# A pad of NOPs on TensorE in three parts, and two weight loads behind a matmul: one change to a gated-linear-attention and feed-forward kernel

## The chip, the cores and the metric

The kernel runs on one core of a Trainium2 chip. The metric is the device time of one execution in microseconds (us), the median of several runs. A core has five engines that run their own instruction streams side by side: TensorE (PE; its weight loads are shown as PEld), VectorE (DVE), ScalarE (ACT), GpSimd (POOL) and SyncE (SP). Here SP asks for all the DMA transfers of data, in program order, on one queue.

## The reference

Two layers, one after the other. The first is a recurrent linear attention with a decay for every key channel; the second is a feed-forward layer with a squared ReLU.

```python
B, H, S, D = 4, 8, 768, 48
for t in range(S):
    state = alpha[:, :, t, :, None] * state + einsum('bhd,bhe->bhde', k[:, :, t], v[:, :, t])
    y[:, :, t] = einsum('bhd,bhde->bhe', q[:, :, t], state)
x = y.transpose(0, 2, 1, 3).reshape(B * S, H * D)      # 3072 x 384
h = maximum(x @ w_in, 0.0)                              # w_in 384 x 2048
out = (h * h) @ w_out                                   # w_out 2048 x 384
```

w_in and w_out come as 64-bit floats, q, k, v and alpha as 32-bit floats.

## The kernel before

**Blocks and groups.** The sequence is cut into chunks of 128 steps; a chunk of one batch element is a block n (24 blocks, n = 0 to 23). A block's attention is made of small products: `cs` (running sums of the logarithms of alpha), `turn` or `kT`/`qT` (transposes, tiles T, kT, qT), `scores` and `state_sums` (tile sckv), and `ga`/`gb` or `joined` (tile y). Four blocks make a group g of 512 rows of x (g = 0 to 5), and the feed-forward layer runs group by group: `ffn_in`, `half_in` or `layer_in` for h, and `layer_out` for the output.

**Products of two kinds.** In group 0, and in part of group 1, products are plain: one 32-bit product is two passes on TensorE. `out_plain` (line 832, products at L816, `o<-w_out,hid`) is such a stage, and in group 1 the first four of the eight pieces of w_out go through it. All other products of groups 1 to 5 use three parts of each factor: `in_x` (the parts a and l; L733, `h<-xa,wb` and `h<-xl,wl`), then `in_y` two steps later (the part d, `h<-xd,wd`). Between the two, ACT scales the sum: L748 or L750. The parts of the weights are made by ACT and DVE in group 1, stored in DRAM, and from then on they are streamed in by SP (L699, wl and wd) when a tile comes free.

**The order of work.** Nothing is scheduled at run time; the program is written out at build time. Up to the first whole products of group 0 a string (`AT['first']`) lists the steps, word by word: `fill1` is a product of zeros on TensorE (L395, tile zeros) whose result nobody reads, `weights3` asks for the next eighth of the weights (the number is not used: the pieces come in order), `load3v` asks for v of block 3, `first`, `middle` and `sga`/`sgb`/`sgc` are the steps in which DVE (L163, L167), ACT (L177, L180) and DVE (L187, L197, L206) turn a piece from 64-bit to 32-bit words. After that, `weave` runs through the list of products (units with a cost each) and puts the other steps (events with a due time) between them. A group's events are dated from `base[g]`, the sum of costs up to the group's start.

**The pad.** `align(place)` (line 1009) writes one instruction into TensorE's program that stands for as many NOPs as it takes until the next instruction is number `place` modulo 256. In the kernel before it is called from `attention`, 2.2 units ahead of the transposes of blocks 4, 14 and 16 (`AT['places']` and `AT['before']`). The three pads come to 59, 78 and 22 NOPs. The pad of 78 stands in group 2, between the sixth product of a step of `in_x` and the first product of the next `in_y`.

**The first SP transfers around the change** are, in order: a piece of w_in (the second), v_in of block 3, the third and the fourth piece of w_in, k_in, q_in and v_in of blocks 5, 4 and 4, and the fifth piece. `dep(later, earlier)` (line 489) makes one instruction wait for another on a semaphore.

Of the kernel before, what the change touches and what calls it, by code (L numbers as in the profile page):

```python
# [15 lines left out]


GB = 4
AT = {'v_by': (2.5, 3.5, 5.0), 'before': 2.2, 'places': ((4, 203), (14, 178), (16, 188)), 'evs': 0.65, 'lead': 4, 'post': 3, 'w_first': (45.25, 42.0, 55.95), 'wstep': 1.6, 'w_in_at': 2.5, 'w_in_by': 3.4, 'room1': 22, 'room': 25, 's0': 4, 'ahead': 6, 'late': 2, 'xs': 0.2, 'g0': ((1.5, 4, False, True, 28.25), (20.25, 6, True, True), (28.75, 8, True, False)), 'sc0': (2.35, 2.35, 2.35), 'g1': ((5.5, 8, False, 15.5), (15.5, 10, True), (34.5, 12, True)), 'g': ((1.7, 6, True), (15.5, 8, True)), 'g1x': 50.0, 'gx': 48.25, 'g0x': 55.25, 'k0': 2, 'h0': 16, 'k1': 4, 'h1': 3, 'h1by': 2, 'evs0': 0.3, 'tp': 'ADMD', 'tp1': 'ADAD', 'split': 8, 'o0': (44.75, 47.25), 'o1': (), 'o2': (21.75, 27.5, 31.75, 35.0, 41.25, 41.75), 'str1': 22.0, 'ga': 9.5, 'gb': 13.0, 'cv0': 1.5, 'first': 'ln0 warm0 cs0 load0v load2a ei0 load1v eb0 mk0 ln1 fill1 fill1 kT0 cs1 kc0 eb1 mq0 qT0 mq1 ei1 qc0 fill1 mk1 fill1 lt0 sc0 lt1 kT1 kv0 qT1 am0 ln2 weights2 us0 load2q kc1 qc1 cs2 sc1 fill1 am1 load2k ei2 load3a eb2 load4a fill1 kv1 st0 first0 us1 fill1 middle0 ln3 mq2 load3k ya0 qT2 yb0 mk2 fill1 qc2 kT2 cs3 kc2 load3q load2v weights5 sc2 eb3 load3v fill1 sga0 weights3 sgb0 fill1 ei3 ev0 mq3 mk3 am2 fill1 qT3 kT3 sgc0 first1 kc3 qc3 middle1 kv2 weights4 ha0 sc3 us2 kv3 sga1 ha1 am3 us3 sgb1 load4k ya2 load4q load4v first2 yb2 sgc1 middle2 weights6 lt3 ev2 lt2 st2 ha3 ha2 sgb2 sga2 hb1 sgc2 hb0 hb2 weights1 st1 hb3 st3 weights0'}


RUN = {0: 128, 32: 32, 64: 64, 96: 32}
# [3 lines left out]
def kernel(  # L26
# [12 lines left out]
    nc = tc.nc  # L39
# [41 lines left out]
    def two_k(name, dt=FP32, shape=(GB * C,)):  # L81
        return two_pool.tile([128, *shape], dt, tag="two", name=name)
# [12 lines left out]
    for x, n in (("q", 2), ("q", 3), ("k", 3)):  # L95
        t = lent[x, n] = two_k("qk_lent", shape=(H, 64))
# [29 lines left out]
    def load_weights(i):  # L126
        dt = moe_w_in.dtype
        shape = (KM, DF // NW) if i < NW else (NJ // NW, DM)
        if dt == FP32:
            raw = target(i)  # L130
        else:
            raw = raw_pool.tile([128, *shape], dt, tag="raw", name="raw")
        raws[i] = raw
        if i < NW:
            src = moe_w_in[:, i * DF // NW : (i + 1) * DF // NW]
            nc.sync.dma_start(out=raw, in_=src.rearrange("(k r) f -> r k f", r=128))
        else:
            i -= NW
            src = moe_w_out[i * DF // NW : (i + 1) * DF // NW, :]
            nc.sync.dma_start(out=raw, in_=src.rearrange("(j r) m -> r j m", r=128))  # L140


    half = {}
# [96 lines left out]
    last = consts.tile([128, 4, NP], FP32, name="last")  # L240
# [23 lines left out]
    def bank(n, name, shape=(NP, C)):  # L264

        return ps_att.tile([128, *shape], FP32, tag="att", name=name)
# [10 lines left out]

    SPLIT = AT["split"]

# [109 lines left out]
        (copied if n < GB else turned_copied)("k", n)  # L389


    def fill(k):
        ps = bank(0, "zeros", (2 * NP, 64))
        for _ in range(k):
            nc.tensor.matmul(  # L395
                out=ps[:, 0:NP, :], lhsT=s_t[3].rearrange("a p d -> a (p d)")[:, 0:128],
                rhs=s_t[3], start=True, stop=True,
            )
# [250 lines left out]
    here, todo, room = {}, [], [22]  # L649
# [28 lines left out]
    def diff_w(w, p):  # L678
# [97 lines left out]
    def splits_of_x(at, g):  # L776
        return [(at + i * AT["xs"], f, (g, i % KM)) for i, f in enumerate((split_x,) * KM + (diff_x,) * KM)]

    def layer_in(g):
        units = []  # L780
        for n in range(NJ + 2):
            if n < NJ:
                units.append((1.05, in_x, (n,)))
            if 0 <= n - 2 < NJ:
                units.append((0.53, in_y, (n - 2,)))
            if 0 <= n - AT["post"] < NJ:
                units.append((0, in_post, (n - AT["post"],)))
# [219 lines left out]
    places = dict(AT["places"])  # L1007
# [118 lines left out]
    for g in range(1, NG):  # L1126
        base.append(begin + sum(u[0] for u in units))
        at0 = base[g]
        units.append((0, begun, (g,)))
        units += layer_in(g) + layer_out(g)  # L1130
        units.append((0, ended, (g,)))
        if g + 1 < NG:
            for t, n0, after, *other in AT["g1"] if g == 1 else AT["g"]:
                n0 = n0 if g == 1 else n0 + GB * g
                other = [None if x is None else at0 + x for x in other]
                events += attention(at0 + t, n0, after, 1, True, *other)
            events += [(at0 + t, f, x) for t, f, x in splits_of_x(AT["g1x" if g == 1 else "gx"], g + 1)]
# [12 lines left out]

# [28 lines left out]
```

## Time and profile before

| | us |
|---|---|
| median of 3 runs | 522.24 (522.23 to 522.29) |
| the profiled execution | 521.93 |
| its span, from first to last instruction | 520.1 |
| TensorE busy in the span | 511.3 |
| DVE, ACT busy | 362.3, 315.6 |

TensorE's granted clock was 0.999 of full speed over the whole span. The profile is of one execution. A row of the timeline gives start, length, engine, line, operation, output and inputs, and in brackets how long the engine stood idle before it and which engine ended that idle time. "issue" means that the profile shows nothing that the engine waited for. PEldq is TensorE's sequencer. In group 0 to 5, L926 and L733 are the products into h, L816 those into the output.

### The profile page before, as it was taken

What the parts mean: (1) busy time and instruction counts of PE and PEld (TensorE: products, weight loads), DVE (VectorE), ACT (ScalarE), POOL (GpSimd) and SP (SyncE); (2) the same over time, 40 slices, a digit from 0 to 9 for tenths busy, and PEclk for the clock granted to TensorE, in tenths of its full rate; (3) what the DMA queues carried; (4) which work ended last, traced back from release to release, by engine and by line L of the source; (5) the groups of instructions that cost most, each with busy time, mean ns of one, the idle gap of its engine ahead of it and who ended that gap; (6) DMA issues with size and microseconds to landing.
All of it is one profiled execution on the core that took longest, in us unless ns stands there. A gap on an engine that the chain in (4) does not pass through costs nothing.

```text
span 520.1 us, 13202 instructions
## 1 busy us (share of the span) xinstructions
PE 511.3 (98%) x5350; PEld 421.9 (81%) x5350; DVE 362.3 (70%) x629; ACT 315.6 (61%) x664; POOL 5.3 (1%) x29
## 2 busy tenths in 40 slices
PE   8999999999999999989999999999999999999997
PEld 6775446668887669968899988899988899988997
DVE  3987979999879579757596466696465485363861
ACT  5678893687999566466953266962266863164620
POOL 4000000000000000000000000000000000000000
PEclk9999999999999999999999999999999999999999
DMA  9999686417888496998885796955683534798201
GB/s 185 214 269 253 180 209 180 67 61 231 242 229 199 121 279 162 309 306 227 183 238 163 245 268 185 227 174 163 214 273 123 182 123 153 252 355 294 70 0 62
DMA packets 139324, 102.36 MB, mean 197 GB/s; under 512 B 109808, under 2 KB 112896, under 8 KB 139264
## 3 DMA queue, kind: packets, MB, share of 16 engines
q1 hardware_dynamic: 139264, 101.52, 68.5%
q8 instruction: 43, 0.70, 0.5%
q14 instruction: 17, 0.14, 0.1%
HBM read 84.17 MB, written 17.33 MB: 195 GB/s over the span
## 4 chain that ended last, share of the span: by engine, by line
PE 92%; DVE 3%; ACT 2%; DMA 1%; issue 1%; SPq 0%; DVEq 0%; POOLq 0%
PE o L816 40%; PE h L733 31%; PE h L926 8%; PE y L409 4%; PE sckv L429 2%; PE T L586 2%; PE sckv L457 2%; DMA a_in<-in_alpha_dram 1%; ACT x L624 1%; PE cs L296 1%; PE cs L299 1%; PE cs L300 1%; DVE x L624 0%; DVE osb L656 0%; DVE xl L656 0%
## 5 line engine op out<-in xcount | busy, mean ns | idle before, releaser
L733 PE MATMUL h<-xa,wb 128*128 128x512 f32 x240 | 69.2, 396 | 0.0
L733 PE MATMUL h<-xd,wd 128*128 128x512 f32 x240 | 66.9, 394 | 1.8 <-ACT ha L706 1.7
L733 PE MATMUL h<-xl,wl 128*128 128x512 f32 x240 | 68.2, 392 | 0.0
L750 ACT ACTIVATE h<-h 128x512 f32<-128x512 f32 x40 | 23.3, 582 | 57.5 <-PE h L733 57.3
L656 DVE TENSOR_TENSOR hid<-h,hid 128x512 f32<-128x512 f32 x40 | 27.5, 688 | 42.7 <-PE h L733 39.9
L624 ACT COPY x<-y 32x256 f32<-32x256 f32 (+2 forms) x132 | 47.1, 364 | 15.2 <-PE y L409 13.0
L816 PE MATMUL o<-wb,ha 128*128 128x384 f32 x160 | 54.2, 339 | 0.0
L733 PEld LDWEIGHTS h<-xd,wd 128*128 128x128 f32 x240 | 44.4, 188 | 11.6 <-ACT ha L706 2.1
L816 PE MATMUL o<-wd,hd 128*128 128x384 f32 x304 | 53.7, 335 | 0.0
L816 PE MATMUL o<-wl,hl 128*128 128x384 f32 x160 | 53.6, 335 | 0.0
L816 PE MATMUL o<-w_out,hid 128*128 128x384 f32 x160 | 53.5, 490 | 0.0
L733 PEld LDWEIGHTS h<-xl,wl 128*128 128x128 f32 x240 | 44.9, 188 | 10.5 <-ACT wl L675 0.6
L816 PEld LDWEIGHTS o<-wd,hd 128*128 128x128 f32 x304 | 52.8, 188 | 0.0
L733 PEld LDWEIGHTS h<-xa,wb 128*128 128x128 f32 x240 | 44.3, 188 | 9.5 <-ACT xa L706 0.3
L816 PE MATMUL o<-wb,hx 128*128 128x384 f32 x144 | 48.8, 339 | 0.0
L816 PE MATMUL o<-wl,hx 128*128 128x384 f32 x144 | 48.2, 335 | 0.0
L816 PEld LDWEIGHTS o<-w_out,hid 128*128 128x128 f32 x160 | 30.0, 190 | 19.6
L926 PE MATMUL h<-x,w_in 128*128 128x512 f32 (+1 forms) x120 | 42.8, 510 | 0.2 <-DVE w_in L206 0.2
L706 ACT ACTIVATE ha<-hid 128x512 fp32r<-128x512 f32 x40 | 25.5, 636 | 23.8 <-DVE hx L656 13.1
L748 ACT ACTIVATE hid<-h 128x512 f32<-128x512 f32 x40 | 24.2, 606 | 25.2 <-PE h L733 25.1
L926 PEld LDWEIGHTS h<-x,w_in 128*128 128x128 f32 x120 | 22.5, 190 | 17.2 <-issue 14.2
L656 DVE TENSOR_TENSOR hl<-hid,ha 128x512 fp32r<-128x512 f32 x40 | 27.5, 686 | 11.2 <-ACT ha L706 11.2
(115 smaller groups left out, 883.7 us busy)
## 6 DMA issues: line engine op xcount, KB each, us to landing
wd<-do SPq DMA_DIRECT2D x36, 384.0 KB
wl<-lo SPq DMA_DIRECT2D x34, 384.0 KB
wl<-li SPq DMA_DIRECT2D x32, 384.0 KB
wd<-di SPq DMA_DIRECT2D x32, 384.0 KB
raw<-in_moe_w_in_dram SPq DMA_DIRECT2D x8, 768.0 KB
raw<-in_moe_w_out_dram SPq DMA_DIRECT2D x8, 768.0 KB
v_in<-in_v_dram SPq DMA_DIRECT2D x24, 192.0 KB
out_dram<-osb SPq DMA_DIRECT2D x24, 192.0 KB
```

Source lines behind the costliest of these rows:

```text
L409: ins = nc.tensor.matmul(out=ys[e][64 * half : 64 * half + D + G * e, m % 2, p // 2, t], lhsT=lhsT, rhs=rhs, start=(half, e) not in seen, ...
L429: nc.tensor.matmul(out=ps[e][HALF[h], 0, p, :], lhsT=ks[rows, p, HALF[h]], rhs=qs[rows, p, HALF[h]], start=True, stop=True, skip_group_che ...
L457: nc.tensor.matmul(out=ps[h][64 * e : 64 * (e + 1), 1, p, G:64], lhsT=tile_of("k", n)[HALF[h], 2 * p + e, :], rhs=tiles["v"][n % NV][HALF[ ...
L586: nc.tensor.transpose(out=ps[h][:, i, p, :], in_=rows[HALF[h], 128 * p : 128 * (p + 1)], identity=ident[HALF[h], HALF[h]],)
L624: copy(out=x[kk][to : to + m, t : t + 2], in_=blk[n]["y"][e][r : r + m, :, p // 2],)
L656: nc.vector.tensor_tensor(out=o, in0=x, in1=z, op=op)
L706: nc.scalar.activation(out=a, in_=x, func=AF.Copy, scale=NEAR)
L733: nc.tensor.matmul(out=acc["h", j], lhsT=here[w, "i", p][:, kk, jj * 128 : (jj + 1) * 128], rhs=x_parts[x][:, kk], start=start and kk == 0 ...
L748: nc.scalar.activation(out=hid[j], in_=x, func=AF.Copy, scale=E)
L750: nc.scalar.activation(out=x, in_=x, func=AF.Copy, scale=1.0 + E)
L816: nc.tensor.matmul(out=acc[t][:, 0:DM], lhsT=lhs[:, t * C : (t + 1) * C], rhs=rhs, start=start, stop=stop, skip_group_check=True,)
L926: nc.tensor.matmul(out=ps, lhsT=w[:, kk, c0 : c0 + 128], rhs=xT[g][kk][:, cols], start=(kk == 0), stop=(kk == KM - 1),)
```

## The change

It has two parts. In the first, `AT['places']` loses the entry for block 14, and a new tuple `pads` lists three calls of `align` as (group, time in the group, place): (1, 33.0, 218), (2, 0.5, 83) and (2, 5.5, 178). They are added to the events before `weave`. The last place, 178, is that of the old pad. In the second part, the word `weights3` leaves the list of first steps between `sga0` and `sgb0`, and a new word, `late0`, comes in behind `am2 fill1` and ahead of `qT3`. It asks for the same piece of w_in, the third, and makes that transfer wait for the last product of zeros written so far. For this, `load_weights` returns its DMA and `fill` keeps its last product. The order of the transfers on SP's queue stays the same.

```diff
-AT = {... 'places': ((4, 203), (14, 178), (16, 188)), ...
+AT = {... 'places': ((4, 203), (16, 188)), 'pads': ((1, 33.0, 218), (2, 0.5, 83), (2, 5.5, 178)), ...
-  'first': '... load3v fill1 sga0 weights3 sgb0 fill1 ei3 ev0 mq3 mk3 am2 fill1 qT3 kT3 ...'
+  'first': '... load3v fill1 sga0 sgb0 fill1 ei3 ev0 mq3 mk3 am2 fill1 late0 qT3 kT3 ...'
...
-            nc.sync.dma_start(out=raw, in_=src.rearrange("(k r) f -> r k f", r=128))
+            ins = nc.sync.dma_start(out=raw, in_=src.rearrange("(k r) f -> r k f", r=128))
...
+        return ins
...
+    zeros = {}
+
     def fill(k):
         ps = bank(0, "zeros", (2 * NP, 64))
         for _ in range(k):
-            nc.tensor.matmul(
+            zeros["last"] = nc.tensor.matmul(
...
+    steps["late"] = lambda _: dep(load_weights(to_load.pop(0)), zeros["last"])
...
+    events += [(base[g] + t, align, (place,)) for g, t, place in AT["pads"]]
     weave(units, sorted(events, key=lambda x: x[0]), begin)
```

More of the change, by code (lines that the diff above doesn't have):

```diff
@@ L18 @@
 GB = 4
-AT = {'v_by': (2.5, 3.5, 5.0), 'before': 2.2, 'places': ((4, 203), (14, 178), (16, 188)), 'evs': 0.65, 'lead': 4, 'post': 3, 'w_first': (45.25, 42.0, 55.95), 'wstep': 1.6, 'w_in_at': 2.5, 'w_in_by': 3.4, 'room1': 22, 'room': 25, 's0': 4, 'ahead': 6, 'late': 2, 'xs': 0.2, 'g0': ((1.5, 4, False, True, 28.25), (20.25, 6, True, True), (28.75, 8, True, False)), 'sc0': (2.35, 2.35, 2.35), 'g1': ((5.5, 8, False, 15.5), (15.5, 10, True), (34.5, 12, True)), 'g': ((1.7, 6, True), (15.5, 8, True)), 'g1x': 50.0, 'gx': 48.25, 'g0x': 55.25, 'k0': 2, 'h0': 16, 'k1': 4, 'h1': 3, 'h1by': 2, 'evs0': 0.3, 'tp': 'ADMD', 'tp1': 'ADAD', 'split': 8, 'o0': (44.75, 47.25), 'o1': (), 'o2': (21.75, 27.5, 31.75, 35.0, 41.25, 41.75), 'str1': 22.0, 'ga': 9.5, 'gb': 13.0, 'cv0': 1.5, 'first': 'ln0 warm0 cs0 load0v load2a ei0 load1v eb0 mk0 ln1 fill1 fill1 kT0 cs1 kc0 eb1 mq0 qT0 mq1 ei1 qc0 fill1 mk1 fill1 lt0 sc0 lt1 kT1 kv0 qT1 am0 ln2 weights2 us0 load2q kc1 qc1 cs2 sc1 fill1 am1 load2k ei2 load3a eb2 load4a fill1 kv1 st0 first0 us1 fill1 middle0 ln3 mq2 load3k ya0 qT2 yb0 mk2 fill1 qc2 kT2 cs3 kc2 load3q load2v weights5 sc2 eb3 load3v fill1 sga0 weights3 sgb0 fill1 ei3 ev0 mq3 mk3 am2 fill1 qT3 kT3 sgc0 first1 kc3 qc3 middle1 kv2 weights4 ha0 sc3 us2 kv3 sga1 ha1 am3 us3 sgb1 load4k ya2 load4q load4v first2 yb2 sgc1 middle2 weights6 lt3 ev2 lt2 st2 ha3 ha2 sgb2 sga2 hb1 sgc2 hb0 hb2 weights1 st1 hb3 st3 weights0'}
@@ new lines @@
+AT = {'v_by': (2.5, 3.5, 5.0), 'before': 2.2, 'places': ((4, 203), (16, 188)), 'pads': ((1, 33.0, 218), (2, 0.5, 83), (2, 5.5, 178)), 'evs': 0.65, 'lead': 4, 'post': 3, 'w_first': (45.25, 42.0, 55.95), 'wstep': 1.6, 'w_in_at': 2.5, 'w_in_by': 3.4, 'room1': 22, 'room': 25, 's0': 4, 'ahead': 6, 'late': 2, 'xs': 0.2, 'g0': ((1.5, 4, False, True, 28.25), (20.25, 6, True, True), (28.75, 8, True, False)), 'sc0': (2.35, 2.35, 2.35), 'g1': ((5.5, 8, False, 15.5), (15.5, 10, True), (34.5, 12, True)), 'g': ((1.7, 6, True), (15.5, 8, True)), 'g1x': 50.0, 'gx': 48.25, 'g0x': 55.25, 'k0': 2, 'h0': 16, 'k1': 4, 'h1': 3, 'h1by': 2, 'evs0': 0.3, 'tp': 'ADMD', 'tp1': 'ADAD', 'split': 8, 'o0': (44.75, 47.25), 'o1': (), 'o2': (21.75, 27.5, 31.75, 35.0, 41.25, 41.75), 'str1': 22.0, 'ga': 9.5, 'gb': 13.0, 'cv0': 1.5, 'first': 'ln0 warm0 cs0 load0v load2a ei0 load1v eb0 mk0 ln1 fill1 fill1 kT0 cs1 kc0 eb1 mq0 qT0 mq1 ei1 qc0 fill1 mk1 fill1 lt0 sc0 lt1 kT1 kv0 qT1 am0 ln2 weights2 us0 load2q kc1 qc1 cs2 sc1 fill1 am1 load2k ei2 load3a eb2 load4a fill1 kv1 st0 first0 us1 fill1 middle0 ln3 mq2 load3k ya0 qT2 yb0 mk2 fill1 qc2 kT2 cs3 kc2 load3q load2v weights5 sc2 eb3 load3v fill1 sga0 sgb0 fill1 ei3 ev0 mq3 mk3 am2 fill1 late0 qT3 kT3 sgc0 first1 kc3 qc3 middle1 kv2 weights4 ha0 sc3 us2 kv3 sga1 ha1 am3 us3 sgb1 load4k ya2 load4q load4v first2 yb2 sgc1 middle2 weights6 lt3 ev2 lt2 st2 ha3 ha2 sgb2 sga2 hb1 sgc2 hb0 hb2 weights1 st1 hb3 st3 weights0'}
@@ L139, in load_weights @@
             src = moe_w_out[i * DF // NW : (i + 1) * DF // NW, :]
-            nc.sync.dma_start(out=raw, in_=src.rearrange("(j r) m -> r j m", r=128))
+            ins = nc.sync.dma_start(out=raw, in_=src.rearrange("(j r) m -> r j m", r=128))
+        return ins
     half = {}
```

## The prediction

> **What bounds the kernel now.** I read the page first: which engine fills the span, and on which engine the chain that ended last runs.
>
> ```profile
> span 520.1 us, 13202 instructions
> PE 511.3 (98%) x5350; PEld 421.9 (81%) x5350; DVE 362.3 (70%) x629; ACT 315.6 (61%) x664; POOL 5.3 (1%) x29
> q8 instruction: 43, 0.70, 0.5%
> PE 92%; DVE 3%; ACT 2%; DMA 1%; issue 1%; SPq 0%; DVEq 0%; POOLq 0%
> ```
>
> TensorE is the bound: busy 511.3 of 520.1 us and 92% of the chain. The change removes no product, so all that it can win lies in the 8.8 us in which TensorE stands. The third line matters later: TensorE's program is fetched while it runs. 5350 products and 5350 weight loads, 159 NOPs and 136 waits that the program holds are 10,995 instructions, and 10,995 / 256 = 43, the number of packets on that queue (0.70 MB / 43 = 16 KB each). So one packet brings a block of 256 instructions, and a slot in the pad's code is a place in such a block.
>
> Next the waits of TensorE alone, longest first, and the chain in order of time (start, length, what).
>
> ```profile
> PE h L733 <- ACT ha L706: 1.7, 1, 1.7
> PE y L409 <- issue: 0.7, 1, 0.7
> ...
> 214.71 6.17 PE h L733 x27
> 296.08 6.17 PE h L733 x27
> 375.47 6.17 PE h L733 x27
> ```
>
> The two waits are the two places that the diff touches. The three chain rows are the starts of groups 2, 3 and 4. Group 2 lasts 296.08 - 214.71 = 81.37 us, group 3 lasts 79.39: the same work, 1.98 us apart.
>
> **Part 1: the pad.** First its NOPs (the rows of line 1011 in three stretches of time; count, then first and last start), then the timeline around the second pad, then busy time by stretch: the opening of groups 2, 3 and 4 up to the chain's T at 228.35, 307.76 and 387.15 (length, PE, PEld, DVE, ACT, POOL).
>
> ```profile
> L1011 PEldq NOP  x59: 13/13/13, 50.3 to 54.6; - x59
> L1011 PEldq NOP  x78: 13/13/13, 219.6 to 225.2; - x78
> L1011 PEldq NOP  x22: 13/13/13, 248.4 to 250.0; - x22
> ...
> 218.87 0.58 ACT L750 ACTIVATE h<-h 128x512 f32<-128x512 f32 x1 [0.76 <-PE h L733]
> 222.81 0.86 PE L733 MATMUL h<-xl,wl 128*128 128x512 f32 x3
> 225.35 0.94 PE L733 MATMUL h<-xd,wd 128*128 128x512 f32 x3 [1.68 <-ACT ha L706]
> ...
> 214.71:228.35 13.64, 11.96 (x54) 9.37 (x55) 7.42 (x15) 7.47 (x16) 0.00 (x0) 1.00 1.01 343
> 296.08:307.76 11.68, 11.68 (x54) 9.46 (x55) 6.82 (x15) 7.48 (x16) 0.00 (x0) 1.00 0.87 263
> 375.47:387.15 11.68, 11.68 (x55) 9.45 (x55) 6.82 (x15) 7.48 (x16) 0.00 (x0) 1.00 0.78 261
> ```
>
> A NOP costs the sequencer (225.2 - 219.6) / 77 = 0.073 us. The sequencer reaches the pad at 219.6 while TensorE still has products queued up to 222.81 + 0.86 = 223.67; so the queue covers about 223.7 - 219.6 = 4.1 us, and 78 NOPs last 5.7 us. The rest is the hole before 225.35. The profile names ACT's ha as releaser, because it ended just then (the pad's end is 225.2); but the product that comes next adds to the sum that ACT's L750 scaled at 218.87, 6.5 us earlier. I therefore put the hole down to the pad. The stretch rows price it without that argument: 13.64 - 11.68 = 1.96 us, and the two openings without a pad have TensorE busy in 11.68 of 11.68 us, with the same attention events and the same streamed weights. So what would be late next is known from group 3: nothing.
>
> Pieces of the new pad: the program holds 2805 TensorE instructions between the first pad (slot 203) and the new place at slot 218, then 863 to slot 83, then 69 to slot 178. 218 - 203 - 2805, 83 - 218 - 863 and 178 - 83 - 69 are each 26 modulo 256. So 78 = 26 + 26 + 26, each 26 x 0.073 = 1.9 us, and from slot 178 on every instruction stands where it stood. Whether 1.9 us is covered, piece by piece:
>
> ```profile
> 178.76 7.58 PE L816 MATMUL o<-w_out,hid 128*128 128x384 f32 x23
> 215.93 0.85 PE L733 MATMUL h<-xa,wb 128*128 128x512 f32 x3
> ```
>
> The first piece lies in the plain products, eight products (sixteen matmuls) ahead of cs at 185.9; one matmul there takes 7.58 / 23 = 0.33 us, so the same number of queued instructions covers more than behind 0.23 us products. It hides. The third is at the old place: 1.9 of 4.1 us. It hides. The second stands between the first and the second in_x, just ahead of the product at 215.93. There the sequencer has just passed the waits for the first loaded wl piece; if it was held there, the queue behind it is shorter than 4.1 us. From the 22 NOPs (1.6 us, 248.4 to 250.0) and the 59 NOPs (4.3 us) I take such lengths as hidden, and 0.6 us as what may show of the second piece. Term: -1.96 us, at worst -1.3.
>
> **Part 2: the order on the SP queue.** It keeps every transfer in its place; the third w_in piece now waits for the last of the zero products ahead of qT3, and behind it on that queue stand the fourth piece, then k_in, q_in and v_in of later blocks, and the fifth piece.
>
> ```profile
> 18.76 2.33 SPq L136 DMA_DIRECT2D raw<-in_moe_w_in_dram  x1
> 21.66 1.16 SPq L136 DMA_DIRECT2D raw<-in_moe_w_in_dram  x2
> 22.11 1.56 PE L395 MATMUL zeros<-s 128*128 128x256 f32 x6
> 29.41 0.33 PE L409 MATMUL y<-qs,us 48*48 48x64 f32 x7
> 29.84 0.55 DVE L163 TENSOR_SCALAR power<-raw 128x768 uint32<-128x768 uint32 x1
> 30.49 0.58 PE L409 MATMUL y<-qs,us 48*64 48x64 f32 x25 [0.75 <-issue]
> 30.49 0.44 PEld L409 LDWEIGHTS y<-qs,us 48*48 48x48 f32 x24 [0.88 <-issue]
> 32.42 2.65 DVE L624 COPY x<-y 32x256 f32<-32x256 f32 x6 [0.69 <-PE y L409]
> 32.86 0.32 ACT L357 COPY last<-lastT 48x4 f32<-48x4 f32 x2 [0.71 <-PE lastT L350]
> 33.10 3.07 PE L926 MATMUL h<-x,w_in 128*128 128x256 f32 x13
> ...
> 22.00:24.00 2.00, 2.00 (x24) 1.73 (x16) 1.96 (x6) 1.92 (x6) 0.00 (x0) 1.00 0.86 259
> 24.00:26.00 2.00, 1.78 (x40) 1.47 (x39) 1.91 (x5) 1.62 (x5) 0.00 (x0) 1.00 1.13 335
> 26.00:28.00 2.00, 2.00 (x70) 1.56 (x68) 1.57 (x3) 1.97 (x4) 0.00 (x0) 1.00 1.07 394
> ...
> q8 instruction: 1, 0.02, 34.0%
> q8 instruction: 1, 0.02, 92.8%
> ```
>
> The last two rows are the DMA queues of 27.8 to 28.0 and of 31.6 to 31.7 (share of 16 engines): a fetch that starts at about 27.9 and takes 0.34 x 16 x 0.2 = 1.09 us, and one at 31.6 of 0.928 x 16 x 0.1 = 1.48 us. Counted back from slot 203, the product at 30.49 is the first instruction of a block. So the 0.75 us "issue" is TensorE waiting for its program: the block was fetched at 27.9 to 29.0 and ran 1.5 us later. The block before it began among the six zeros matmuls, at 22.3 to 22.6, so its successor was due to be asked for then, and got its turn 5 us later. In between, the DMA engines were full (335 and 394 GB/s in the stretches from 24 and 26 on) with the second and the third w_in piece, asked for at 18.76 and 21.66. With the third asked for only after 22.11 + 1.56 = 23.67, 2.0 us later, the fetch stands ahead of it; it should then start at about 26 and be usable at 26 + 1.1 + 1.5 = 28.6, before 29.5. The hole goes: 0.75 us of TensorE idle, 0.88 us by the weight loads.
>
> How much of it stays won has two limits. TensorE's next users do not all follow: the x copies on DVE and the copy on ACT waited 0.69 and 0.71 us for TensorE, so they can come at most 0.7 us earlier. And the next block's fetch is itself just in time: 31.6 + 1.48 + up to 1.5 = 34.6 us, while its first instruction, 256 on, is the seventh of the h products, at 33.10 + 6.5 x 0.215 = 34.5 us. If TensorE arrives 0.9 us earlier and that fetch does not move, TensorE waits there again. It is asked for at the crossing, which moves from 30.49 to about 29.5, but into the tail of the delayed fourth piece. Between 0 and -0.9 us I take the middle, -0.45.
>
> The delay itself I cost at nothing. From 22.0 on the engines still have the second piece (0.79 MB) and a v load (0.20 MB): 0.52 MB go by 24.0, the rest at 335 GB/s by 25.4, so the queue hardly runs dry before the third piece, asked for at 23.7, arrives. It then lands near 26 + 0.79 / 0.38 = 28.1 us, and DVE reads it at 29.84. Without that cover DVE's conversions would be late and each us of it would cost up to one us at the next h products.
>
> [...]
>
> **Sum.** -1.96 - 0.45 = -2.4 us on the profiled execution, 521.93 to 519.5; it is 0.31 us below the median of the runs, so 522.24 becomes 519.8 us. Three runs lie within 0.06 us; a change under 0.2% (1.0 us) counts as none.
>
> **Rivals.**
> *The fetch stays late* (the next block takes the gain back, or the third piece was not what held it): only part 1 counts, 522.24 - 1.96 = 520.3. For it: the just-in-time fetch at 31.6. Against it: 5 us from crossing to fetch just while the w_in pieces fill the engines. Chance 0.25. [...]
> *The blocks' borders move into a bad place.* Between the first and the second piece all instructions stand 26 slots later, so four borders (in program order near 186, 198, 204.5 and 210.6 us) fall 26 instructions earlier in the work. One that is reached before its fetch, as at 30.49, costs 0.75 to 0.9 us: 520.7. Against it: each of these blocks lasts 6 us or more, because each holds long products. Chance 0.06.
> *The hole is ACT's,* as the profile's releaser has it: then parting the pad wins nothing there, and only part 2 counts, 522.24 - 0.45 = 521.8. Chance 0.03: groups 3 and 4 have the same ACT work (7.48 us in the stretch) and no hole. [...]
> *The NOPs are not covered* (slower): if the sequencer is held by a wait right ahead of each piece, the queue is empty and each shows its whole 1.9 us: 5.7 in place of 1.96, 522.24 + 3.7 = 526.0. It decides from two uncovered pieces on; one alone (1.9) leaves about today's time. For it: the second piece follows waits for loads. Against it: the first and the third stand in steady products. Chance 0.05 for slower, 0.03 for one piece.
>
> The forecast has the remaining 0.58. The range runs from 522.24 - 1.3 = 520.9, part 1 at its worst and nothing from part 2, to both holes in full, 522.24 - 1.98 - 0.9 = 519.4, widened by the 0.3 us between profile and median: 519.0 to 520.9, rounded down. Faster 0.89 (the forecast and the first two rivals), same 0.06 (ACT's hole, one piece uncovered), slower 0.05.
>
> **What would show it.** Right: line 1011 in three lots of 26 in group 1's plain products, at the opening of group 2 and at the old place, with TensorE's busy time equal to the stretch; group 2 as long as group 3; no "issue" row at y L409 and an instruction packet at about 26. Wrong: a PE wait at h L733 near 216 or 222, a new "issue" row at h L926 near 34, or a DVE L163 that waits for raw.

## The result, and the profile after

The changed kernel takes 521.03 us (median of 22 runs, 520.10 to 523.05); the kernel before, run beside it, 522.34 (521.88 to 524.17). The ratio is 0.9975, interval 0.9966 to 0.9984: 1.3 us faster, where 2.4 were forecast, and just outside the range of 519.0 to 520.9. In two later comparisons the ratio was 0.9973 (0.9959 to 0.9988) and 0.9972 (0.9961 to 0.9983). The profiled execution took 520.71 us, 1.22 less than that of before.

Line numbers of the changed kernel: L395, L409, L487, L586, L733, L816, L926 and L1011 became L398, L412, L490, L589, L736, L819, L929 and L1016. The page first (span, busy time, shares of the chain):

```profile
span 518.9 us, 13202 instructions
PE 512.0 (99%) x5350; PEld 422.0 (81%) x5350; DVE 362.1 (70%) x629; ACT 316.2 (61%) x664; POOL 5.3 (1%) x29
PE 93%; DVE 2%; ACT 2%; DMA 1%; SPq 0%; issue 0%; POOL 0%; DVEq 0%; POOLq 0%
```

TensorE is still the bound. The NOPs of the three pieces, each from a stretch of its own (count, first and last start):

```profile
L1016 PEldq NOP  x26: 13/13/13, 176.0 to 177.9; - x26
L1016 PEldq NOP  x26: 13/13/13, 213.5 to 215.3; - x26
L1016 PEldq NOP  x26: 13/13/13, 220.0 to 221.8; - x26
```

The starts of groups 2, 3 and 4 in the chain:

```profile
214.90 6.35 PE h L736 x27
294.88 6.17 PE h L736 x27
374.26 6.17 PE h L736 x27
```

Busy time by stretch for the openings of groups 2 and 3 (length, PE, PEld, DVE, ACT, POOL, clock, DMA share, GB/s):

```profile
214.90:226.76 11.86, 11.86 (x54) 9.37 (x55) 6.92 (x15) 7.49 (x16) 0.00 (x0) 1.00 0.98 341
294.88:306.56 11.68, 11.68 (x55) 9.44 (x55) 6.82 (x15) 7.47 (x16) 0.00 (x0) 1.00 0.89 265
```

The three pieces are where they were meant to be, and in this execution none shows: TensorE is busy in 11.86 of 11.86 us. The opening lost 13.64 - 11.86 = 1.78 us. But group 2 now starts at 214.90, 0.19 later than before, and from T to the end of the span there are 518.9 - 226.76 = 292.14 us, where there were 520.1 - 228.35 = 291.75: 0.39 longer. 1.78 - 0.19 - 0.39 = 1.20, the difference of the spans. Group 2 as a whole lasts 294.88 - 214.90 = 79.98 us and group 3 79.38, where the prediction had them equal. So one reading gives two losses, one ahead of group 2 and one behind its opening. Both have rows. The start, weight loads that TensorE waited for (start, length, in brackets the idle time):

```profile
29.44 0.69 PEld L412 LDWEIGHTS y<-qs,us 48*48 48x48 f32 x32 [0.33 <-issue]
34.65 1.91 PEld L929 LDWEIGHTS h<-x,w_in 128*128 128x128 f32 x9 [0.98 <-issue]
```

The hole at 30.49 is gone (the 0.33 at 29.44 was there before as well), and in its place stands one of 0.98 us at the h products, exactly one block of 256 instructions later. Behind the opening, in group 2's second stretch of attention:

```profile
239.25 0.36 DVE L490 TENSOR_TENSOR s<-s,last 128x192 f32<-128x192 f32 x1 [2.88 <-DMA last<-row]
239.53 0.68 DVE L768 SCALAR_TENSOR_TENSOR hid<-hid 128x512 f32<-128x512 f32 x1
240.13 0.68 DVE L659 TENSOR_TENSOR hid<-h,hid 128x512 f32<-128x512 f32 x1
```

And TensorE in the same timeline:

```profile
240.87 0.96 PE L736 MATMUL h<-xa,wb 128*128 128x512 f32 x3 [0.21 <-DVE hid L659]
```

VectorE waits 2.88 us for `last`, the decay row of block 14 or 15, which goes to DRAM and back; everything behind it on VectorE is late, and TensorE, which needs the buffer that L659 frees, loses 0.28 us there (0.42 from one product to the next, usually 0.14). In the kernel before, VectorE waited 1.68 us at the same place and TensorE nothing:

```profile
239.65 0.36 DVE L487 TENSOR_TENSOR s<-s,last 128x192 f32<-128x192 f32 x1 [1.68 <-DMA last<-row]
```

### The profile page after: what moved, and what is told of

Read it like the earlier page. It is cut to its first block, busy times and chain, and to the rows that moved or that the text cites. A ratio compares the mean times of both kernels' runs of the same rounds, so it can differ in the third digit from the quotient of the medians.

```text
span 518.9 us, 13202 instructions
## 1 busy us (share of the span) xinstructions
PE 512.0 (99%) x5350; PEld 422.0 (81%) x5350; DVE 362.1 (70%) x629; ACT 316.2 (61%) x664; POOL 5.3 (1%) x29
## 4 chain that ended last, share of the span: by engine, by line
PE 93%; DVE 2%; ACT 2%; DMA 1%; SPq 0%; issue 0%; POOL 0%; DVEq 0%; POOLq 0%
PE o L819 40%; PE h L736 31%; PE h L929 7%; PE y L412 4%; PE T L589 2%; PE sckv L432 2%; PE sckv L460 2%; DMA raw<-in_moe_w_in_dram 1%; ACT x L627 1%; PE cs L297 1%; PE warm L251 1%; PE cs L301 1%; PE cs L300 1%; SPq L119 0%; DVE osb L659 0%
## 5 line engine op out<-in xcount | busy, mean ns | idle before, releaser
L736 PE MATMUL h<-xa,wb 128*128 128x512 f32 x240 | 69.1, 396 | 0.2 <-DVE hid L659 0.2
L736 PE MATMUL h<-xl,wl 128*128 128x512 f32 x240 | 68.1, 392 | 0.0
L736 PE MATMUL h<-xd,wd 128*128 128x512 f32 x240 | 66.9, 394 | 0.1
L659 DVE TENSOR_TENSOR hid<-h,hid 128x512 f32<-128x512 f32 x40 | 27.5, 688 | 41.2 <-PE h L736 38.4
L819 PE MATMUL o<-wb,ha 128*128 128x384 f32 x160 | 54.2, 339 | 0.0
L819 PE MATMUL o<-wd,hd 128*128 128x384 f32 x304 | 53.7, 334 | 0.0
L819 PE MATMUL o<-w_out,hid 128*128 128x384 f32 x160 | 53.5, 490 | 0.0
L819 PE MATMUL o<-wl,hl 128*128 128x384 f32 x160 | 53.5, 334 | 0.0
L736 PEld LDWEIGHTS h<-xl,wl 128*128 128x128 f32 x240 | 44.9, 188 | 10.5 <-ACT wl L678 0.6
L819 PEld LDWEIGHTS o<-wd,hd 128*128 128x128 f32 x304 | 52.8, 188 | 0.0
L736 PEld LDWEIGHTS h<-xd,wd 128*128 128x128 f32 x240 | 44.4, 188 | 9.9 <-ACT hid L751 0.8
L736 PEld LDWEIGHTS h<-xa,wb 128*128 128x128 f32 x240 | 44.3, 188 | 9.8 <-ACT xa L709 0.3
L819 PE MATMUL o<-wb,hx 128*128 128x384 f32 x144 | 48.7, 338 | 0.0
L819 PE MATMUL o<-wl,hx 128*128 128x384 f32 x144 | 48.1, 334 | 0.0
L819 PEld LDWEIGHTS o<-w_out,hid 128*128 128x128 f32 x160 | 29.9, 190 | 19.7
L929 PE MATMUL h<-x,w_in 128*128 128x512 f32 (+1 forms) x120 | 42.9, 510 | 1.0 <-ACT x L627 0.8
L929 PEld LDWEIGHTS h<-x,w_in 128*128 128x128 f32 x120 | 22.5, 190 | 18.2 <-issue 15.9
L659 DVE TENSOR_TENSOR hl<-hid,ha 128x512 fp32r<-128x512 f32 x40 | 27.4, 686 | 10.9 <-ACT ha L709 10.8
```

The lines of the kernel that those rows point to most:

```text
L659: nc.vector.tensor_tensor(out=o, in0=x, in1=z, op=op)
L736: nc.tensor.matmul(out=acc["h", j], lhsT=here[w, "i", p][:, kk, jj * 128 : (jj + 1) * 128], rhs=x_parts[x][:, kk], start=start and kk == 0 ...
L819: nc.tensor.matmul(out=acc[t][:, 0:DM], lhsT=lhs[:, t * C : (t + 1) * C], rhs=rhs, start=start, stop=stop, skip_group_check=True,)
L929: nc.tensor.matmul(out=ps, lhsT=w[:, kk, c0 : c0 + 128], rhs=xT[g][kk][:, cols], start=(kk == 0), stop=(kk == KM - 1),)
```

## The experiments

Ratios are to runs of the kernel before beside them on the same chip; 0.001 is 0.52 us, and the brackets hold 95% intervals. Each kernel has one profiled execution. A border is the step in TensorE's program from one block of 256 instructions to the next (in the kernel before, 43 packets of 16,384 bytes brought 10,995 instructions, 255.7 each). "Border stalls" are the idle times of the weight loads put down to "issue" at the y products near 30 us and the h products near 34.5 or a little later (without the 0.33 that all kernels show).

**One part alone.** The two parts apart:

```diff
 pads alone:   'first': the word weights3 back at its old place, no late0
 delay alone:  'places': ((4, 203), (14, 178), (16, 188)), 'pads': ()
```

> The pad in three parts alone; the third w_in piece is asked for at its old place. Theory A (the pad's hole is gone in full; what was lost is at the start, where the next block's fetch takes the first hole's gain back): 522.3 - 1.9 = 520.4 us, runs as close together as those of before (0.4 us), the hole of 0.75 us at y L412 near 29.7 still there, and TensorE without a wait at h L736 near 223. Rival B (the pad's pieces or the borders that moved in group 1 cost something again): 521.2 us or more, with a wait on TensorE between 180 and 230 us or runs spread over 2 us.

> The late third piece alone; the pad of 78 NOPs is whole at its old place. Theory A: 522.3 us within 0.3 in the middle, but runs spread over 1.5 to 2 us, because the length of the new hole near 34 us hangs on when that block's fetch gets its turn; the hole at 223 is there with 1.7 us. Rival B: 521.5 us (0.75 us won at 29.7 and kept), runs close together.

Pads alone: 521.93 us, 0.9989 (0.9975 to 1.0002). Delay alone: 522.96 us, 0.9998 (0.9985 to 1.0011), border stalls 0 and 1.64. So the delay by itself shows no gain (its interval still holds the 0.45 us forecast), and the pads by themselves bring less than 1.96. The two gains together, 0.0011 and 0.0002, make half of the changed kernel's 0.0025 to 0.0028; the intervals are too wide to tell whether that is noise. Why the pads alone bring less, their profile shows. The NOPs of its middle piece:

```profile
L1016 PEldq NOP  x26: 13/13/13, 215.6 to 217.5; - x26
```

and TensorE around them:

```profile
214.84 0.86 PE L736 MATMUL h<-xa,wb 128*128 128x512 f32 x3
215.59 0.92 PE L736 MATMUL h<-xl,wl 128*128 128x512 f32 x3
217.59 0.94 PE L736 MATMUL h<-xa,wb 128*128 128x512 f32 x3 [1.08 <-issue]
```

Here the middle piece begins at 215.6, when TensorE is already in the products with the first streamed wl piece, and shows 1.08 us; in the profile above it began at 213.5 and showed nothing.

**The third piece, the fourth piece, and the loads behind them.** The fourth piece behind the first y product of block 2, too:

```diff
-  ... kv2 weights4 ha0 ... sgb1 load4k ya2 load4q load4v first2 ...
+  ... kv2 ha0 ... sgb1 ya2 behind2 load4k load4q load4v first2 ...
```

> The changed kernel, and the fourth w_in piece (and the k, q and v loads behind it) is asked for only behind the first y product of blocks 2 and 3, that is after the border at 29.5 us. Theory A: the fetch of the next block starts at about 30.3 in place of 31.9, the 0.74 us wait at h near 34 is gone, and the time falls to about 519.8 us with runs close together. Rival B, and a rival C by which a fetch takes its 1.5 us and more whatever stands beside it: the wait near 34 stays and the time is that of the changed kernel, 521.0 us. If the loads behind are then late, a wait for a_in near 45 us or for raw shows.

522.75 us, 0.9991 (0.9977 to 1.0006). The first fetch started at 28.12 (27.29 in the profile of the changed kernel) with a stall of 0.62, although the fourth piece no longer stood there. The second border stalled for 2.07 us, the longest stall of all these kernels. Two stretches of this kernel (the two last numbers are the DMA share and GB/s):

```profile
28.00:31.00 3.00, 2.51 (x66) 1.89 (x61) 2.64 (x6) 1.54 (x5) 0.00 (x0) 1.00 0.04 11
31.00:34.00 3.00, 2.87 (x110) 2.58 (x100) 2.50 (x6) 2.52 (x6) 0.00 (x0) 1.00 0.84 264
```

From 28 to 31 us the DMA engines were all but empty. The fourth piece was asked for at 30.07, k_in, q_in and v_in from 30.53 on; TensorE crossed the border at 30.55, and the fetch started at 34.22 only. By then the fourth piece had been moved (264 GB/s over the second stretch are its 0.79 MB, and it landed at 34.19 to 34.80; the trace has a record for each of the sixteen shares of a transfer), while the three loads landed at 35.28 to 38.37. So this fetch went behind the fourth piece, which had been asked for half a microsecond ahead of the border, and not behind the three loads.

Then the same three loads and the fifth piece, asked for only behind the third h tile:

```diff
-  ... sgb1 load4k ya2 load4q load4v first2 yb2 sgc1 middle2 weights6 lt3 ev2 lt2 st2 ha3 ha2 ...
+  ... sgb1 ya2 first2 yb2 sgc1 middle2 lt3 ev2 lt2 st2 ha3 held0 load4k load4q load4v ha2 ...
```

> The changed kernel, with k_in, q_in and v_in of blocks 5, 4 and 4 and the fifth piece of w_in asked for only when the last product of the third h tile has run (about 34.3 us; before, they were asked for from 24.7 us on). The third and fourth piece stay as they are. Theory A, the next block's fetch waits behind those small transfers: it starts near 29.8 to 30.5 us in place of 31.9, the stall at the h products near 33.5 (0.74 us) goes, and TensorE reaches 46 us some 0.5 to 0.7 us earlier; the time falls by as much, unless the fifth piece, then landing near 38 us, comes too late for VectorE. Theory B, the fetch is not held by transfers but asked for at about 31.8 us whatever is on the queues: it starts at 31.6 to 32.3 as in all runs so far, the stall stays at 0.7 us or more, and the time is the same or longer.

524.09 us, 1.0028 (1.0016 to 1.0041), and yet the second fetch came early, as theory A has it. The instruction packet in the DMA queues of 29.8 to 30.0 us:

```profile
q8 instruction: 1, 0.02, 33.9%
```

and the waits of 44 to 64 us (total, times, longest):

```profile
ACT a_in L275 <- DMA a_in<-in_alpha_dram: 5.0, 1, 5.0
PEld h L929 <- DVE w_in L207: 2.2, 1, 2.2
...
PE T L589 <- DVE q_in L316: 0.9, 1, 0.9
```

The second fetch started at 29.91 (31.86 in the changed kernel), both border stalls were 0, and cs came at 45.53 (46.27). What was moved then came too late itself: alpha's transfer, the fifth piece and q. Against two other kernels that crossed the first border without a stall, with the first fetch nearly as early (25.23 and 25.65, here 24.83) but the three loads asked for ahead of the border, the second fetch is 1.5 us earlier (31.45 and 31.44 there).

**The middle piece and the row transfers.** The changed kernel again, as a mark; the middle piece 24 instructions later; the row transfers on GpSimd's queue:

```diff
 middle later:     'pads': ((1, 33.0, 218), (2, 2.5, 107), (2, 5.5, 178))
 rows on GpSimd:   q = nc.gpsimd if n in (14, 15) else nc.sync      # in bl and br
                   q.dma_start(...)
```

> The changed kernel once more, as the mark for the other three runs. Its gain was about 1.3 us, not 2.4. If its spread comes from the second piece of the pad (shown in full when the first streamed wl piece lands late, hidden otherwise), the profiled execution shows either a hole of about 1.2 us at 216 us or none. In both cases: the start's two stalls at block borders together 0.8 to 0.9 us (y near 29.5 and h near 33.5), and about 0.3 to 0.5 us more than usual between sckv and h near 240.4. Time 521.0, 0.9975 of before.

> The changed kernel, with the middle piece of 26 NOPs one step of in_x later (behind the second one, not behind the first); the two other pieces and all other instructions as in the changed kernel. Theory, the middle piece is only partly covered because the sequencer has just been held by the wait for the first streamed wl piece: 24 instructions later it has its queue again, no hole near 216 in any execution, time 0.3 to 0.6 us below the changed kernel and a narrower spread. Rival, the middle piece is hidden as it stands and the gain is lost elsewhere: the same time as the changed kernel, 521.0, and the same spread.

> The changed kernel, with the four small transfers that bring the last decay row of blocks 14 and 15 to DRAM and back asked for by GpSimd's own queue, in place of SP's, which at that time stands behind a streamed wl piece. Theory, that round trip is what is late next when the pad's hole is gone: VectorE's wait for last<-row near 239 us (2.9 us in the changed kernel, 1.7 before) falls under 1 us, the 0.28 us that TensorE loses near 240.4 goes, time 0.3 us below the changed kernel. Rival, the small transfers are late because the DMA engines are full and not because of SP's queue: the wait stays between 2 and 3 us and the time as it is.

Again: 521.06 us, 0.9973. The same program, now with the hole: its middle piece, the product behind it, and the opening by stretch.

```profile
L1016 PEldq NOP  x26: 13/13/13, 215.3 to 217.3; - x26
```

```profile
217.33 0.94 PE L736 MATMUL h<-xa,wb 128*128 128x512 f32 x3 [0.88 <-PE h L736]
```

```profile
214.90:227.90 13.00, 12.12 (x55) 9.53 (x56) 7.11 (x15) 7.55 (x16) 0.00 (x0) 1.00 0.95 324
```

Middle piece later: 520.82 us, 0.9969 (0.9955 to 0.9983), no hole near 216, and nine of twelve runs within 520.5 to 521.1, where the mark spread from 520.0 to 523.4. The medians differ by 0.24 us in the expected direction, which the intervals do not tell apart. Rows on GpSimd: 520.95 us, 0.9973 (0.9959 to 0.9987). VectorE's wait for `last` is gone, and so is TensorE's loss (the lines of these kernels stand two further down):

```profile
236.26 0.36 DVE L492 TENSOR_TENSOR s<-s,last 128x192 f32<-128x192 f32 x1
```

```profile
240.44 0.97 PE L738 MATMUL h<-xa,wb 128*128 128x512 f32 x3
```

So that round trip was late because of SP's queue. TensorE's loss follows the length of the wait: at 1.68 us (the kernel before) and at 2.32 (the loads behind h, and the second mark further down) it lost nothing, at 2.9 to 3.1 (six profiles) it stood 0.21 to 0.45 us. By the times the repair shows nothing: 520.95 and the mark's 521.06 are one within the noise. Its profiled execution was the shortest of all, 520.51 us. The same edit in the kernel before:

> The kernel before, with nothing changed but the row transfers of blocks 14 and 15 on GpSimd's queue. Theory, this wait costs TensorE nothing as long as the pad's hole stands ahead of it: VectorE's wait for last<-row (1.7 us) goes and the time stays within 0.2 us of before. Rival, it costs there too: 0.3 us faster.

522.59 us against 522.64, 0.9998 (0.9980 to 1.0015): the wait is gone there too, and it was worth nothing while the pad's hole stood ahead of it. It became a loss in profiles without that hole, and not in all of them.

**Both repairs, and the start repaired.** Third run: the fifth piece first and then the small loads, behind the last y product of block 2. Fourth: the same without the delay of the third piece.

```diff
 small loads late:  '... sgb1 ya2 first2 yb2 sgc1 middle2 held0 load4k load4q load4v lt3 ev2 ...'
 without late0:     '... sga0 weights3 sgb0 fill1 ei3 ev0 mq3 mk3 am2 fill1 qT3 ...'
```

> The changed kernel with both repairs: the middle piece of the pad one step of in_x later, and the row transfers of blocks 14 and 15 on GpSimd's queue. Theory, the pad's gain was cut by these two places: no hole near 216, no wait for last<-row near 239, no excess at 240.4; the opening of group 2 and its second attention stretch run as in group 3, and the time is 520.4 (1.96 us of the pad in full, nothing from the start). Rival, the two overlap (an uncovered middle piece gives the row transfers time): no better than either alone, 520.8.

> The same, and the start repaired: the fifth piece of w_in, then k_in, q_in and v_in are asked for behind the last y product of block 2 (near 31.3 us), not before it. Theory, the second fetch was held by the small transfers: it starts near 30 us, no stall at h near 33.5, cs at 45.5 in place of 46.2, and, since the fifth piece is asked for when it was before, nothing of it is given back: 519.7, 0.7 us below the run without it. Rival, the small transfers, now asked for 7 us later, hold the fifth piece's successors or alpha's transfer behind them and TensorE loses it again before 65 us: 520.4 or more.

> As the run before in this list, but with the third piece of w_in asked for at its old place, not behind the zero products: what the second part of the change is worth when the next block's fetch does not take it back. Theory, the third piece does hold the first of the two fetches: it starts near 27.8 us, a stall of 0.4 to 0.9 us at y near 29.5, and the time is 0.45 us longer than with the delay. Rival, the second piece and what was asked for before it hold that fetch: no difference over 0.2 us.

Both repairs: 521.27 us, 0.9968 (0.9955 to 0.9981), not the 520.4 expected. Its profile has a new wait at the opening, for a streamed weight and not for NOPs (its middle piece had ended at 218.2):

```profile
219.88 0.93 PE L738 MATMUL h<-xd,wd 128*128 128x512 f32 x3 [0.36 <-DMA wd<-di]
```

Small loads late: 521.62 us, 0.9976 (0.9965 to 0.9988), so the rival was right on the time: border stalls 0.34 and 0, cs 0.70 earlier than with both repairs alone (46.11 for 46.81, of which it had 0.28 at 17 us already), and 1.36 us lost again up to 131 us, for the most part at T near 61.5 and 90, where VectorE's q_in was late. The second fetch speaks against the theory that the small loads hold it: they had not been asked for yet. It did not start near 30 but at 31.57, 1.1 us after a border that was crossed late (30.48); it took 1.0 us in place of 1.4 to 1.8 and was in time. Without the delay: 522.25 us, 0.9983 (0.9971 to 0.9996), 0.63 us slower by the medians. Its first border:

```profile
30.72 0.58 PE L414 MATMUL y<-qs,us 48*64 48x64 f32 x25 [0.75 <-issue]
```

Its border stalls are 0.88 and 0, against 0.34 and 0: with the next block's stall out of the way, the delay of the third piece is worth about what was forecast, by the medians; the intervals overlap.

**The pad placed otherwise.** The middle piece ahead of the wait for the first wl piece, in the last output products of group 1; that with the rows on GpSimd; that without the delay; and a mark.

```diff
 middle in o:   'pads': ((1, 33.0, 218), (1, 53.0, 53), (2, 5.5, 178))
```

> The changed kernel a third time, the mark for the three runs beside it: 0.9973 to 0.9975 of before. Its profile shows at 216 us either a hole of about 1.1 us, as in the second profile, or none, as in the first.

> The changed kernel with the middle piece of 26 NOPs put into the last output products of group 1 (wd,hd, 0.17 us each, near 212 us), ahead of the wait for the first streamed wl piece and not behind it. Theory, the wait for that piece empties the queue and so shows the middle piece: sixteen queued products of 0.17 us are 2.7 us, more than its 1.9, so no hole near 212, 216 or 219; time 0.3 to 0.6 us below the changed kernel. Rival, TensorE waits for the first wl piece itself when it comes early, so whatever the NOPs free is lost to that load: the same hole at 216 without any NOP there, and the same time.

> As the run before in this list, and the row transfers of blocks 14 and 15 on GpSimd's queue. Theory: both losses of the pad's gain are gone, nothing at 216, 219 or 240.4, and group 2 is as long as group 3 (79.4 us); time 0.6 to 0.9 us below the changed kernel, 0.996 of before. Rival: the row transfers matter only when the middle piece doesn't show, and something else takes its place: the same as the run before.

> As the run before in this list, with the third piece of w_in asked for at its old place: the worth of the second part of the change, measured with the pad's chance gone. Theory, the next block's fetch takes back what the first stall gives: within 0.2 us of the run before. Rival, the delay is worth what was forecast, 0.45 us: slower by that.

Mark: 521.43 us, 0.9972. Middle in o: 521.70, 0.9979 (0.9958 to 1.0001). With the rows: 521.80, 0.9986 (0.9971 to 1.0002). Without the delay: 521.68, 0.9982 (0.9970 to 0.9994); one of its twelve executions took 2,894 us, and nothing on record says why. The theory fell: the piece showed 0.20, 0.59 and 0.37 us between the output products, and in that stretch TensorE also waits for streamed weights (0.25 us for wd at 213.0 in the second run), which may be why the queue is short there. Even the mark, with no NOP there, had its weight loads wait 0.5 us for wd near 212. The last pair has the delay worth nothing, -0.12 us by the medians, as the theory had it.

No middle piece, both ways of sharing the 78, and the whole pad in the plain products; the first two with the rows on GpSimd:

```diff
 26 + 52:        'pads': ((1, 33.0, 218), (2, 5.5, 178))
 52 + 26:        'pads': ((1, 33.0, 244), (2, 5.5, 178))
 78 in group 1:  'pads': ((1, 33.0, 14),)       # without late0
```

> The changed kernel with the pad in two pieces, 26 NOPs in group 1's plain products and 52 at the old place, no middle piece, and the row transfers of blocks 14 and 15 on GpSimd's queue. Theory, the middle piece's exposure (1.05 and 1.24 us in two of the profiles, none in the others) is what spreads the changed kernel, and 52 NOPs (3.8 us) are just covered at the old place, where 78 (5.7) showed 1.85, that is a cover of 3.8 to 3.9: 520.5, 0.9965 of before, with a narrow spread. Rival, the opening of group 2 runs at the pace of the streamed weights, not of TensorE: without the middle piece TensorE waits there for wd or wl (near 212 to 220 us) and the time stays at 0.997 to 0.998 of before.

> As the run before in this list, but 52 NOPs in the plain products and 26 at the old place. In the plain products 78 NOPs showed 0.65 us, so 52 are hidden with 1.3 us to spare, but four block borders stand 52 instructions earlier, and the block from 198.2 to 201.4 us (in the time of the kernel before) lasts only 3.1 us: theory, a stall of 0.1 to 0.6 us at y or o near 201 to 203, where the shift of 78 (a block of 1.8 us) gave 1.4 and that of 26 (5.2 us) none; time 520.5 plus that stall. Rival, only blocks under 2 us stall: the same as the run before in this list or a little better.

> The pad whole, 78 NOPs, at the first new place, in group 1's plain products; third piece at its old place. Theory A (the NOPs hide behind queued products, 16 to 18 of them, each 0.33 us long here): cover of 5.3 to 5.9 us against 5.7, so at most 0.4 us of hole near 184 us and a time of 520.4 to 520.8. A rival by which the cover is a fixed time of 4.1 us: a hole of 1.6 us near 184 and 522 us.

26 + 52: 521.28 us against 523.13, 0.9961 (0.9947 to 0.9975), the best ratio of all, 2.0 us. But its median is not below the marks' 521.03 to 521.43; the kernel before was slower in this comparison than in the others, no mark ran beside it, and the intervals overlap. 52 + 26: 521.57, 0.9969 (0.9953 to 0.9984). 78 in group 1: 522.96, 0.9998 (0.9985 to 1.0012). 26 + 52, at the old place:

```profile
223.97 0.93 PE L738 MATMUL h<-xd,wd 128*128 128x512 f32 x3 [0.29 <-DMA wd<-di]
```

52 + 26, in the last output products of group 1:

```profile
213.56 2.70 PE L821 MATMUL o<-wd,hd 128*128 128x384 f32 x14 [0.81 <-DMA wd<-do]
```

78 in group 1, right behind the pad and at a border behind it:

```profile
182.35 0.88 PE L819 MATMUL o<-w_out,hid 128*128 128x384 f32 x2 [0.48 <-issue]
...
202.72 0.34 PE L412 MATMUL y<-am,v_in 64*64 64x64 f32 x6 [1.19 <-issue]
```

In the first kernel the 52 NOPs ran from 220.1 to 223.86 and the wd load landed at 223.77, so both held the product at 223.97: of the 0.29 the NOPs alone can have cost 0.1 us, and without them TensorE would have waited for the streamed weight, as the rival has it. In the second no border stalled, so the block of 3.1 us held, but TensorE, that much earlier, waited 0.81 us for a streamed wd. In the third 78 NOPs show 0.48 us even behind 0.33 us products, and a border that the shift brought into a block of short products stalled for 1.19.

## Why the prediction was wrong, point by point

**Part 2, the delay: the first hole was priced too high, and the limit that the prediction had named took back all of the gain.** By the five kernels of these rows with the third piece at its old place and the small loads early (before, pads alone, 78 in group 1, before with the rows, middle in o without the delay), the stalls are on average 0.61 at the first border (0.88, 0.62, 0.34, 0.59, 0.60) and 0.40 at the second (0, 0.43, 0.98, 0.43, 0.15). By the eleven with the delay (after and its two marks, delay alone, middle later, rows, both repairs, middle in o without and with the rows, 26 + 52, 52 + 26) they are 0.15 (0.34 in five, 0 in six) and 0.93 (0.98, 0.70, 0.70, 1.64, 0.98, 0.43, 1.12, 0.98, 1.34, 0.70, 0.70). The first border won 0.46, where the prediction took 0.75 to 0.9 us from a single profile, the one with the longest stall of the five; the second lost 0.53, where it took half of the gain, 0.45, as lost. That 0.46 is close to the term of 0.45 is chance, since the term was what should be left over. That is the rival "the fetch stays late (the next block takes the gain back)", to which the prediction gave 0.25, and its sign of being wrong, an "issue" row at h near 34, was seen. The rival's time, 520.3, was missed too, by what part 1 lost. Its just-in-time arithmetic was right: "31.6 + 1.48 + up to 1.5 = 34.6", against 34.65. The step that failed is the middle taken between 0 and -0.9: the crossing did move earlier, but the second fetch did not follow, since it started between 31.4 and 32.4 us in all these sixteen kernels, and at 29.9 in the one that crosses the border without a stall and has not yet asked for k, q and v. In the sixteen it starts between 0.41 us before and 0.01 us after the last of the sixteen landings of the fourth w_in piece, and where that piece was asked for later (the fourth piece behind y) it came later with it. So the tail of the fourth piece, which the prediction had named in passing, is what stood ahead of it; that k, q and v add to it, one kernel suggests (29.9), and two speak against it (31.57 and 31.84 with these loads not yet asked for). The times do not settle what the delay is worth: the pairs of runs with and without it (pads alone, delay alone, small loads late, middle in o) leave between -0.1 and 0.9 us.

Two further steps of this part failed. The first fetch was to start at about 26: in the same kernels it started between 25.2 and 27.8 with the delay (27.29 in the first profile) and 27.6 to 28.1 without, 0.8 us earlier on average and not 2. What else holds it is open: it came late with the fourth piece out of the way (28.12) and with the small loads late (27.99), and early with these later still (24.83). And the delay was costed at nothing for VectorE: it did wait 0.4 us for raw (the waits of 24 to 36 us), which cost TensorE nothing that shows.

**Part 1, the pad.** The hole was the pad's, not ACT's: where the old pad stayed, it stayed (delay alone, and before with the rows), and where only its place changed, ACT's work being the same, it went (pads alone). Two steps of the term were wrong. First, the 0.6 us for the middle piece: it shows either nothing (the profiles of the changed kernel, its second mark, rows on GpSimd, the fourth piece behind y, the loads behind h) or 0.9 to 1.1 us (pads alone, the first mark), and which of the two is seen where its first NOP stands: 1.2 to 1.5 us ahead of the first product of group 2 in the five, 0.45 and 0.77 us behind it in the two. Right ahead of it is the wait for the first streamed wl piece, and the landings in the traces show that it sets the place: in all seven the sequencer passes that wait 0.03 us after the last of the load's sixteen shares has landed, and the first NOP follows 0.15 to 0.20 us after that landing. In the two bad profiles fifteen shares had landed by 213.7, and the last came at 215.2 and 215.5; why one share was late is open. Second, "what would be late next is known from group 3: nothing". In the stretch rows of the prediction group 3's opening has a DMA share of 0.87 and 263 GB/s, group 2's 1.01 and 343, after the change 0.98 and 341. Once TensorE gained its 1.8 us, the transfers were late: `last` by 0.28 us (gone with the rows on GpSimd, harmless before the change and in the second mark), or a streamed wd by 0.2 to 0.8. The rows that priced the hole were right; the DMA share, in the last columns of the same rows, had not been read.

**The other rivals.** The blocks' borders did not move into a bad place with 26, but they did with 78 (1.19 us, where the rival had 0.75 to 0.9). In these rows the cover is a count of queued products more than a time: 78 NOPs at 0.073 us leave 5.7 - 0.48 = 5.2 us covered by products of 0.33 us, and 5.7 - 1.68 = 4.0 by products of 0.23 to 0.29, 14 to 17 products, with their weight loads about 30 instructions, in both.

**The time.** The forecast counted 1.96 + 0.45. The runs have 1.78 of the first in a good execution and 0.9 less in a bad one, less 0.28 to 0.4 behind the opening, and by the profiles about -0.1 to -0.2 for the second: 1.2 to 1.4 in the good ones, which is what the median says, and 0.5 or less in the bad ones (the first mark's profiled execution took 521.93 us, the same as that of before). That these bad ones make much of the spread is likely but not shown, since only one execution of each kernel has a profile.

## What to carry to other kernels

When a stall goes, read the DMA share and the waits of the other engines behind it, not only the next group's busy time: the stall had been giving the transfers time. NOPs, which only the sequencer runs, were hidden here by the products that TensorE still had queued, for up to 4.0 us behind products of 0.23 to 0.29 us and up to 5.2 behind products of 0.33, so put such instructions where nothing has just held the sequencer, and look in several executions where the first of them starts. When one block's fetch comes in time, the next block's is the one to check (with the delay the first stall fell from 0.61 to 0.15 us, and the second rose from 0.40 to 0.93), together with the transfers that were asked for shortly ahead of its border.

## What was not expected of the hardware

In these kernels a fetch of TensorE's program waited behind transfers that had been asked for ahead of its border. Crossed at 30.55 with a piece of 768 KB asked for at 30.07 (the fourth piece behind y), it started 3.7 us later, at 34.22, as that piece landed (34.19 to 34.80), although the engines had been all but empty up to 31 us (a DMA share of 0.04 from 28 us on); with this piece and the small loads asked for some us earlier, 1.1 to 2.3 us later; with the small loads still to come, 0 to 1.1 us later. The piece went as 384 moves of 2 KB, and the fetch did not start before the first of the sixteen shares had landed (34.19). The second border then stalled for 2.07 us, where the prediction had 0.75 to 0.9 us for one that is reached before its fetch.

For most of the 43 blocks of the kernel before the fetch was in time, since TensorE's products have one wait that is put to "issue" (0.75 us); where it was not, the border cost 0.15 to 2.07 us in these kernels. Counted in steps of 256 from the product at 30.49, the program of that kernel has 43 borders and each has one fetch, which starts between 3.5 us ahead of TensorE's crossing and 5.0 us behind it. That some start ahead fits a sequencer that is ahead of TensorE: it came to the 78 NOPs with 4.1 us of products still to run.
